# Turning the first nine and all half expert tiles on TensorE from whole rows, with another pace of the weight loads

## The chip, the cores and the metric

The kernel runs on one core of a Trainium2 chip. The metric is the device time of one execution in microseconds, as the median of three runs. The core's engines are TensorE (PE, with its weight loads as PEld), VectorE (DVE), ScalarE (ACT), GpSimd (POOL) and SyncE (SP); here SyncE issues nearly all ordinary DMAs and GpSimd the indirect ones.

## What is computed

Two layers in a row. The first is a long convolution over 4 sequences of 11456 tokens with 128 channels, done by Fourier transforms of length 2 x 11456 and multiplied by `x`. Its output, 45824 rows of 128, goes into a mixture of 8 experts, where each token takes the one expert with the highest logit:

```python
logits = x @ w_gate + modality_bias[modality_id]
e_idx = np.argmax(logits, axis=1)
probs = softmax(logits); gate_w = probs[np.arange(N), e_idx]
for e in range(E):                      # E = 8, D = 128, F = 1024
    mask = e_idx == e
    h = np.maximum(x[mask] @ w1[e], 0.0)
    out[mask] = gate_w[mask, None] * (h @ w2[e])
```

All of it is in fp32.

## The kernel before

The first half of the time (up to about 1100 us) is the convolution, with the routing of each sequence running one sequence behind. The routing puts each token's row into `xs` in HBM, sorted by expert. A row of `xs` has `RW = 130` numbers: 128 channels, the gate and the token's number. GpSimd writes these rows with indirect DMAs (`send_rows`, L269), and keeps doing so into the second half for the later sequences.

The second half is `experts(0, 99)` (L981). It goes over 99 tiles: 82 of `T = 512` rows, then 17 of `TH = 256` rows, the half tiles (up to five more half tiles lie behind a condition that does not hold with these inputs). Each tile belongs to one expert, which is read from a table at run time. The loop body is one chunk (`at`): a full tile has eight chunks `c`, a half tile four. In each chunk the order of the program, which is also the order of each engine's queue for TensorE, ScalarE, VectorE and SyncE, is: rows of tile `i + 2` are loaded if `c` is 0 (`rows_in`), `hidden(at)`, whole weights if due, one quarter of the weights of tile `i + 1` (`weights`, `c < 4`), `result(at - 3)`, and at fixed chunks `rows_turn(i + 1)`, `rows_split(i + 1)` and `rows_out(i - 1)`. GpSimd's order is found by the compiler's own planning.

- fp32 products are made of three matmuls on halves of the number, a high part (`h`, fp32r) and a low part (`l`, the rest). `weights` (L1049) makes them: ScalarE casts to `wh` (L1069), VectorE subtracts to `wl` (L1071); for half tiles the subtractions of parts 1 and 3 go to GpSimd. For the first `NDYN = 8` tiles the raw weights of the tile's expert are loaded just for it (`w1r`, `w2r`, L1028 and L1030, two buffers each); from tile 8 on they come from `w1a`, `w2a`, all experts' weights kept in SBUF, which `whole_weights` (L1041) loads in 16 DMAs of 512 KB, one in each odd chunk from tile 2 on.
- `rows_in` loads 512 rows so that VectorE's 32 x 32 transpose (L1088) gives channels on partitions: four DMAs in runs of 32 numbers (L1005), and one of the two last numbers of each row into `ends` (L1007). `rows_split` makes `xh` (ScalarE, L1096) and `xl` (VectorE, L1097).
- `hidden` makes `ph` (L1110 to L1112), then the relu `hh` on ScalarE (L1115) and `hl` on VectorE (L1116). `result` adds up `po` (L1133 to L1135) over the tile. After the last chunk VectorE transposes `po` to `oT` (L1141), four DMAs store it in short runs to `ob` in HBM (L1145), and one DMA reads it back as rows, `y` (L1147).
- `rows_out` casts the token numbers (`idx`, L1156), multiplies `y` by the gate on GpSimd (L1163) and scatters the rows to `out` by indirect DMAs, 128 rows each (L1165). Only the last tile is turned back by TensorE: `oT` by ScalarE (L1139), `pe.transpose` (L1160), the product on VectorE (L1161).

PSUM has eight banks, taken in turn by `bank(...)`. `x` and `ot` have four buffers, `ends` eight. `finale` (the end of the last routing) runs in tiles 0 and 1.

Of the kernel before, what the change touches and what calls it, by code (L numbers as in the profile page):

```python
# [12 lines left out]
F32 = mybir.dt.float32  # L13
# [22 lines left out]
B, S, D, E, F = 4, 11456, 128, 8, 1024  # L36
# [7 lines left out]
T = 512  # L44
# [11 lines left out]
RW = D + 2  # L56
# [11 lines left out]
TG, FL = 18, 2  # L68
NDYN = 8
NA, NXO = 11, 3  # L70


def places():
# [106 lines left out]
def hyena_moe_kernel(ctx: ExitStack, tc: tile.TileContext, a: dict, out: bass.AP,  # L180
                     nb: int = B, nt: int = NF + NH):
    nc = tc.nc
    pe, act, dve, pool, sp = nc.tensor, nc.scalar, nc.vector, nc.gpsimd, nc.sync
# [14 lines left out]
    def bank(name):  # L198
        return banks[-1].tile([D, 512], F32, tag="ps", name=name)
# [781 lines left out]
    def experts(lo, hi):  # L981
# [3 lines left out]
        last = hi - 1  # L985

        def rows_in(i):
            if i > last:
                return
            tb, col, n = tiles[i]  # L990
            for gen in {"1": (), "b": (second,)}.get(tb, (second, others)):
                for _ in gen:
                    pass
            tab = tabs[tb]
            r = nc.values_load(tab[0:1, 0, col:col + 1], engines=[ENG.SP], min_val=0, max_val=E * R,
                               skip_runtime_bounds_check_because="clamped above")
            k = kept[i] = {"n": n}

            x = k["x"] = mt.tile([D, T // 32, 32], F32, tag="x", name="x", bufs=4)
            ends = k["ends"] = mt.tile([D, 4, 2], F32, tag="ends", name="ends", bufs=8)  # L1000

            def rows():

                of = xs[ds(r, n), 0:D].rearrange("(f t) (k e) -> k t f e", t=32, e=32)
                lds = [sp.dma_start(x[32 * j:32 * j + 32, 0:n // 32], of[j]) for j in range(4)]  # L1005
                way = "(j p) r -> p j r" if i == last else "(p j) r -> p j r"
                lds.append(sp.dma_start(ends[:, 0:n // D],  # L1007
                                        xs[ds(r, n), D:RW].rearrange(way, j=n // D)))
                if tb in ("1", "b"):

                    known = max(nb - (2 if tb == "1" else 1), 0) * NR // D
                    assert len(scatters) >= known
                    for ld in lds:
                        for s in scatters[known:]:
                            tc.declare_no_dep(ins_of(ld), s, reason="rows of later tiles")
                        after_all(ld, scatters[:known])

            def raw_weights():

                e = nc.values_load(tab[0:1, 2, col:col + 1], engines=[ENG.SP], min_val=0, max_val=E - 1,  # L1020
                                   skip_runtime_bounds_check_because="clamped above")
# [12 lines left out]
            for part in of[:1] + [rows] + of[1:] if i == 0 else [rows] + of:  # L1034
                part()
            if i < NDYN:
                k["w", 1] = k["w", 1].rearrange("p c d -> p (c d)")
            if i == NDYN:
                whole_weights(2 * E)
# [9 lines left out]
        def weights(i, part):  # L1049
# [17 lines left out]
            else:  # L1067
                src = wv[m][:, ds(k["e"] + at, half)]
            act.copy(k[m, "h"][:, at:at + half], src)  # L1069
            eng = pool if k["n"] < T and part % 2 else dve  # L1070
            eng.tensor_sub(k[m, "l"][:, at:at + half], src, k[m, "h"][:, at:at + half].bitcast(F32))  # L1071

        def turn_tiles(i):

            k = kept[i]
            k["idx"] = mt.tile([D, 4], I32, tag="idx", name="idx", bufs=10)
            k["xT"] = mt.tile([D, T], F32, tag="xT", name="xT")
            k["xh"] = mt.tile([D, T], F32R, tag="xh", name="xh")
            k["xl"] = mt.tile([D, T], F32R, tag="xl", name="xl")

        def rows_turn(i):
            if i > last:
                return
            k = kept[i]
            n = k["n"]
            if "idx" not in k:
                turn_tiles(i)
            dve.transpose(k["xT"][:, 0:n], k["x"].rearrange("p f e -> p (f e)")[:, 0:n])  # L1088

        def rows_split(i):  # L1090
            if i > last:
# [27 lines left out]
        def result(at):  # L1119
# [15 lines left out]
                pe.matmul(po, k[1, "h"][:, f], hl[:, t], start=False, stop=g == NCH - 1)  # L1135
            if g == NCH - 1:
                oT = k["oT"] = mt.tile([D, T], F32, tag="oT", name="oT")
                if i == last:
                    act.copy(oT[:, 0:n], po)  # L1139
                    return  # L1140
                dve.transpose(oT[:, 0:n], po)  # L1141
                ob = ob_t[i % 4]
                to = ob[0:n].rearrange("(f t) (k e) -> k t f e", t=32, e=32)
                for j in range(4):
                    sp.dma_start(to[j], oT[32 * j:32 * j + 32, 0:n].rearrange("p (f e) -> p f e", e=32))  # L1145
                y = k["y"] = mt.tile([D, 4, D], F32, tag="y", name="y", bufs=2)
                sp.dma_start(y[:, 0:n // D], ob[0:n].rearrange("(p j) d -> p j d", j=n // D))  # L1147

        def rows_out(i):
            if not lo <= i <= last:  # L1150
# [1 line left out]
            k = kept.pop(i)  # L1152
            n = k["n"]
            ot = mt.tile([D, T], F32, tag="ot", name="ot", bufs=4).rearrange("p (j d) -> p j d", d=D)
            gate = k["ends"][:, 0:n // D, 0:1].broadcast_to([D, n // D, D])
            pool.tensor_copy(k["idx"][:, 0:n // D], k["ends"][:, 0:n // D, 1])  # L1156
            if i == last:
                pt = bank("pt")
                for j in range(n // D):
                    pe.transpose(pt[:, D * j:D * j + D], k["oT"][:, D * j:D * j + D], ident)  # L1160
                dve.tensor_mul(ot[:, 0:n // D], pt[:, 0:n].rearrange("p (j d) -> p j d", d=D), gate)  # L1161
            else:
                pool.tensor_mul(ot[:, 0:n // D], k["y"][:, 0:n // D], gate)  # L1163
            for j in range(n // D):
                s = pool.indirect_dma_start(  # L1165
                    out=out, out_offset=bass.IndirectOffsetOnAxis(ap=k["idx"][:, j:j + 1], axis=0),
# [10 lines left out]
        for at in range(len(work) + 6):  # L1177
# [9 lines left out]
                fetched.append(fetch(nb - 1))  # L1187
            if lo == 0 and 3 * at % 10 < 3:
                send_rows(1)
            if lo == 0 and 2 <= i and c % 2:  # L1190
                whole_weights(1)
            if 8 <= i < NW0:
                next(second, 0)
# [3 lines left out]
                weights(i + 1, c)  # L1197
            result(at - 3)
            whole = i <= last and tiles[i][2] == T
            if c == (3 if whole else 0):  # L1200
                rows_turn(i + 1)
            if c == (4 if whole else 1):
                rows_split(i + 1)
            if c == (5 if whole else 3):
                rows_out(i - 1)
# [50 lines left out]
```

## Time and profile before

| | us |
|---|---|
| median of 3 runs (2195.53 to 2204.09) | 2199.9 |
| the profiled execution | 2179.15 |
| its span, first to last instruction | 2177.3 |

| engine | busy, us | share of the span |
|---|---|---|
| PE | 2053.4 | 94% |
| PEld | 1662.4 | 76% |
| DVE | 1720.4 | 79% |
| ACT | 1183.9 | 54% |
| POOL | 1236.6 | 57% |

The share of busy time is an average over stages. The expert tiles are therefore read one by one: a tile lasts from its first `ph` matmul (L1110) to the next tile's, and the trace is cut there. In the view by stretches, a line gives the stretch in us from the span's start, its length, then for PE, PEld, DVE, ACT and POOL the busy time and in brackets the number of instructions, then the granted share of TensorE's clock (1.00 is 2.4 GHz, 0.5 would be 1.2 GHz throughout), the mean busy share of the 16 DMA engines and the GB/s that they moved. In the view of waits, a line names who waited, for whom, the total in us, how many times and the longest. In the timeline a line has the start, the length, engine, source line, operation, out<-in, how many were merged, and in square brackets the idle time before it and what ended it.

### The profile page before, as it was taken

The numbers are of one execution on the slowest core, as the hardware profiler recorded it, in microseconds if no ns is written. First come the engines' busy times: TensorE is split into PE (matmuls) and PEld (weight loads), VectorE is DVE, ScalarE is ACT, GpSimd is POOL, SyncE is SP. The second block draws the span as 40 slices with busy tenths as digits, with TensorE's granted clock in tenths as the row PEclk, the third lists the DMA queues.
The fourth block names the chain that finished last, engine by engine and source line by source line (L and its number), as shares of the span: only waits on it lengthen the run. The fifth ranks groups of instructions, "written<-read, shape, count | busy, mean of one in ns | idle before, by whom it ended". The sixth has DMA issues, their size and how long they took to land. (4 is left out here: it accounts for less than half of the span.)

```text
span 2177.3 us, 50618 instructions
## 1 busy us (share of the span) xinstructions
PE 2053.4 (94%) x18024; PEld 1662.4 (76%) x18024; DVE 1720.4 (79%) x2813; ACT 1183.9 (54%) x2155; POOL 1236.6 (57%) x1263
## 2 busy tenths in 40 slices
PE   8989999899989999899986899999999999999985
PEld 8878777677767777686565688888888888888884
DVE  2349777896789767996884899998899998889873
ACT  4642366225642366225653666666666666666653
POOL 0216400596448854596434578777777465554785
PEclk9999999999999999999998999999999999999997
DMA  9577677777878788785688766666665555555432
GB/s 313 219 286 229 236 231 217 236 256 271 303 258 271 269 284 302 247 263 164 191 197 225 174 134 133 127 125 131 124 130 116 114 102 98 98 97 94 81 69 54
DMA packets 592747, 406.51 MB, mean 187 GB/s; under 512 B 455977, under 2 KB 489469, under 8 KB 592489
## 3 DMA queue, kind: packets, MB, share of 16 engines
q1 hardware_dynamic: 565833, 343.82, 58.6%
q0 software_dynamic: 26496, 59.36, 7.9%
q8 instruction: 144, 2.36, 0.5%
q14 instruction: 114, 0.93, 0.1%
q10 hardware_dynamic: 160, 0.03, 0.0%
HBM read 295.03 MB, written 108.42 MB: 185 GB/s over the span
## 5 line engine op out<-in xcount | busy, mean ns | idle before, releaser
L1116 DVE SCALAR_TENSOR_TENSOR hl<-ph,hh 128x512 fp32r<-128x512 f32 x724 | 480.0, 675 | 74.4 <-ACT hh L1115 67.6
L269 POOL DMA_INDIRECT xs<-back,to x360 | 369.8, 1027 | 257.9 <-DVE y L675 83.0
L1115 ACT ACTIVATE hh<-ph 128x512 fp32r<-128x512 f32 x724 | 423.0, 598 | 168.3 <-PE ph L1112 161.8
L1165 POOL DMA_INDIRECT out<-ot,idx x362 | 400.9, 1107 | 110.4 <-issue 76.9
L1133 PE MATMUL po<-hh,wh 128*128 128x512 f32 (+1 forms) x792 | 297.2, 375 | 22.9 <-ACT hh L1115 22.9
L1110 PE MATMUL ph<-xh,wh 128*128 128x512 f32 (+1 forms) x792 | 297.4, 376 | 17.5 <-ACT xh L1096 17.5
L1112 PE MATMUL ph<-xl,wh 128*128 128x512 f32 (+1 forms) x792 | 297.4, 376 | 2.1 <-DVE xl L1097 2.1
L1134 PE MATMUL po<-hh,wl 128*128 128x512 f32 (+1 forms) x792 | 295.9, 374 | 2.9 <-POOL wl L1071 2.9
L1135 PE MATMUL po<-hl,wh 128*128 128x512 f32 (+1 forms) x792 | 296.3, 374 | 1.4 <-DVE hl L1116 1.1
L1111 PE MATMUL ph<-xh,wl 128*128 128x512 f32 (+1 forms) x792 | 296.3, 374 | 0.7 <-POOL wl L1071 0.7
L643 ACT COPY A<-pw 128x512 f32<-128x512 f32 (+1 forms) x184 | 97.1, 579 | 347.3 <-PE pw L639 347.3
L615 DVE TENSOR_TENSOR part<-pz,rings 128x1024 f32<-128x1024 f32 (+1 forms) x184 | 211.4, 1189 | 1.7 <-POOL part L620 1.7
L610 POOL TENSOR_TENSOR more<-more 128x256 f32<-128x256 f32 (+1 forms) x92 | 72.5, 788 | 233.1 <-DVE more L608 228.9
L639 PEld LDWEIGHTS pw<-rings,part 64*128 64x128 f32 x2880 | 175.5, 188 | 35.2 <-issue 28.4
L639 PE MATMUL pw<-rings,part 64*128 64x128 f32 x2880 | 200.3, 278 | 2.0 <-POOL part L620 1.9
L1163 POOL TENSOR_TENSOR ot<-y,ends 128x512 f32<-128x512 f32 (+1 forms) x98 | 104.4, 1065 | 167.7 <-DMA y<-ob 166.7
L596 PE MATMUL pz<-A,rings 128*64 128x256 f32 x1440 | 177.9, 389 | 15.1 <-DMA rings<-in_c_b 9.1
L1133 PEld LDWEIGHTS po<-hh,wh 128*128 128x128 f32 x792 | 151.2, 191 | 50.5 <-ACT hh L1115 24.6
L1110 PEld LDWEIGHTS ph<-xh,wh 128*128 128x128 f32 x792 | 151.1, 191 | 44.4 <-ACT xh L1096 19.1
L464 PE MATMUL s<-fwd,seq 128*64 128x90 f32 x4096 | 170.7, 242 | 6.0 <-issue 4.6
L1112 PEld LDWEIGHTS ph<-xl,wh 128*128 128x128 f32 x792 | 151.0, 191 | 30.7 <-DVE xl L1097 4.9
L1135 PEld LDWEIGHTS po<-hl,wh 128*128 128x128 f32 x792 | 150.7, 190 | 30.2 <-DVE hl L1116 4.6
(182 smaller groups left out, 3742.4 us busy)
## 6 DMA issues: line engine op xcount, KB each, us to landing
rings<-hs SPq DMA_DIRECT2D x88, 512.0 KB
seq<-in_u SPq DMA_DIRECT2D x64, 512.0 KB
seq<-in_v SPq DMA_DIRECT2D x64, 512.0 KB
seq<-in_x SPq DMA_DIRECT2D x64, 512.0 KB
xr<-xo SPq DMA_DIRECT2D x64, 365.6 KB
back<-xr SPq DMA_DIRECT2D x72, 325.0 KB
rings<-in_c_b SPq DMA_DIRECT2D x88, 256.0 KB
rings<-in_c_c SPq DMA_DIRECT2D x88, 256.0 KB
```

The lines of the kernel that those rows point to most:

```text
L269: s = pool.indirect_dma_start(out=xs, out_offset=bass.IndirectOffsetOnAxis(ap=ix, axis=0), in_=src, in_offset=None, bounds_check=E * R - 1 ...
L615: dve.tensor_mul(part[i], z[:, :, i].unsqueeze(1).broadcast_to([D, 2, n, 2, D]), h[:, 0].unsqueeze(3).broadcast_to([D, 2, n, 2, D]))
L639: pe.matmul(pw[par][:, to:to + D], t[at], k["c"][at, q, c], start=i == 0, stop=i == len(terms) - 1)
L1110: pe.matmul(p, k[0, "h"][:, f:f + D], k["xh"], start=True, stop=False)
L1111: pe.matmul(p, k[0, "l"][:, f:f + D], k["xh"], start=False, stop=False)
L1112: pe.matmul(p, k[0, "h"][:, f:f + D], k["xl"], start=False, stop=True)
L1115: act.activation(hh, ph, AF.Relu)
L1116: dve.scalar_tensor_tensor(hl, ph, 0.0, hh.bitcast(F32), op0=ALU.max, op1=ALU.subtract)
L1133: pe.matmul(po, k[1, "h"][:, f], hh[:, t], start=g == 0, stop=False)
L1134: pe.matmul(po, k[1, "l"][:, f], hh[:, t], start=False, stop=False)
L1135: pe.matmul(po, k[1, "h"][:, f], hl[:, t], start=False, stop=g == NCH - 1)
L1165: s = pool.indirect_dma_start(out=out, out_offset=bass.IndirectOffsetOnAxis(ap=k["idx"][:, j:j + 1], axis=0), in_=ot[:, j, :], in_offset=N ...
```

## The change

`NPE = 9`. A tile is `by_pe` if it is one of the first nine, the last, or a half tile. For such a tile:

- its rows are loaded whole, 130 numbers each, in one DMA into `x` (`[D, 4, RW]`), and `ends` is a part of that tile;
- `rows_turn` has TensorE transpose `x` (four or, in a half tile, two transposes of 128 x 128 with the identity) into a PSUM bank `px`, from which `rows_split` reads;
- `po` is copied to `oT` by ScalarE, transposed by TensorE into `pt` in `rows_out`, and multiplied by the gate on VectorE. `ob` and `y` are not used.

The other tiles, 9 to 81, do as before. For half tiles only part 3 of the low weights is on GpSimd (it was 1 and 3); their `rows_turn` is in chunk 1 (it was 0) and `rows_split` in chunk 2 (it was 1). The whole weights are loaded in chunks 0, 3 and 6 from tile 1 on.

```diff
+NPE = 9
...
-            x = k["x"] = mt.tile([D, T // 32, 32], F32, tag="x", name="x", bufs=4)
-            ends = k["ends"] = mt.tile([D, 4, 2], F32, tag="ends", name="ends", bufs=8)
+            by_pe = k["by_pe"] = i < NPE or i == last or n < T
+            x = mt.tile([D, 4, RW], F32, tag="x", name="x", bufs=4)
+            if by_pe:
+                k["x"], k["ends"] = x, x[:, :, D:RW]
+            else:
+                k["x"] = x.rearrange("p j r -> p (j r)")[:, 0:T]
+                k["ends"] = mt.tile([D, 4, 2], F32, tag="ends", name="ends", bufs=8)
...
+                by_token = xs[ds(r, n), :].rearrange("(p j) r -> p j r", j=n // D)
+                if by_pe:
+                    lds = [sp.dma_start(x[:, 0:n // D], by_token)]
+                else:
+                    of = xs[ds(r, n), 0:D].rearrange("(f t) (k e) -> k t f e", t=32, e=32)
+                    to = k["x"].rearrange("p (f e) -> p f e", e=32)
+                    lds = [sp.dma_start(to[32 * j:32 * j + 32], of[j]) for j in range(4)]
+                    lds.append(sp.dma_start(k["ends"], by_token[:, :, D:RW]))
...
-            eng = pool if k["n"] < T and part % 2 else dve
+            eng = pool if k["n"] < T and part == 3 else dve
...
-            dve.transpose(k["xT"][:, 0:n], k["x"].rearrange("p f e -> p (f e)")[:, 0:n])
+            if k["by_pe"]:
+                k["xT"] = bank("px")
+                for j in range(n // D):
+                    pe.transpose(k["xT"][:, D * j:D * j + D], k["x"][:, j, 0:D], ident)
+            else:
+                dve.transpose(k["xT"], k["x"])
...
-                if i == last:
+                if k["by_pe"]:
                     act.copy(oT[:, 0:n], po)
                     return
...
-            if i == last:
-                pt = bank("pt")
+            if k["by_pe"]:
+                pt = bank("pt").rearrange("p (j d) -> p j d", d=D)
                 for j in range(n // D):
-                    pe.transpose(pt[:, D * j:D * j + D], k["oT"][:, D * j:D * j + D], ident)
-                dve.tensor_mul(ot[:, 0:n // D], pt[:, 0:n].rearrange("p (j d) -> p j d", d=D), gate)
+                    pe.transpose(pt[:, j], k["oT"][:, D * j:D * j + D], ident)
+                dve.tensor_mul(ot[:, 0:n // D], pt[:, 0:n // D], gate.broadcast_to([D, n // D, D]))
             else:
-                pool.tensor_mul(ot[:, 0:n // D], k["y"][:, 0:n // D], gate)
+                pool.tensor_mul(ot, k["y"], gate.broadcast_to([D, 4, D]))
...
-            if lo == 0 and 2 <= i and c % 2:
+            if lo == 0 and 1 <= i and c % 3 == 0:
                 whole_weights(1)
...
-            if c == (3 if whole else 0):
+            if c == (3 if whole else 1):
                 rows_turn(i + 1)
-            if c == (4 if whole else 1):
+            if c == (4 if whole else 2):
                 rows_split(i + 1)
```

## Rows read from the trace of the kernel before

**Rows 1.** Busy time by stretch, cut at tiles; columns explained above.

```profile
1100.01:1113.79 13.78, 13.78 (x71) 10.48 (x72) 11.90 (x22) 10.45 (x21) 3.46 (x4) 0.88 0.95 245
...
1113.79:1126.29 12.50, 11.75 (x53) 9.07 (x52) 11.14 (x27) 6.19 (x12) 2.69 (x3) 1.00 0.76 200
...
1148.32:1168.05 19.73, 12.70 (x49) 9.72 (x48) 9.45 (x16) 7.07 (x15) 8.17 (x9) 0.83 0.86 222
...
1168.05:1190.46 22.41, 13.81 (x50) 10.71 (x48) 10.49 (x18) 7.76 (x15) 7.37 (x8) 0.77 0.87 227
...
1190.46:1208.78 18.32, 12.67 (x49) 9.91 (x48) 8.24 (x15) 6.38 (x13) 8.10 (x9) 0.81 0.89 225
...
1233.71:1244.59 10.88, 10.88 (x49) 9.01 (x48) 10.35 (x22) 6.91 (x14) 8.97 (x9) 1.00 0.76 152
...
1908.27:1951.79 43.52, 43.52 (x193) 36.05 (x192) 38.84 (x60) 29.44 (x53) 24.68 (x24) 1.00 0.53 98
...
2064.14:2069.89 5.75, 5.75 (x50) 5.75 (x49) 5.75 (x8) 3.58 (x8) 5.28 (x7) 1.00 0.39 55
...
2027.95:2144.47 116.52, 101.40 (x760) 96.92 (x759) 89.10 (x140) 71.35 (x142) 95.47 (x103) 0.96 0.39 75
```

**Rows 2.** Waits in tiles 3 to 7: total us, times, longest.

```profile
ACT wh L1069 <- DMA w1r<-in_moe_w: 34.6, 4, 12.2
...
PE po L1133 <- ACT hh L1115: 22.9, 4, 8.6
```

**Rows 3.** SyncE's own waits in tiles 3 to 7, same columns.

```profile
SPq L1147 <- DMA ob<-oT: 20.0, 7, 4.6
```

**Rows 4.** Timeline, tile 5: SyncE, then ScalarE; start, us, instruction, [idle before].

```profile
1170.38 6.43 SPq L1005 DMA_DIRECT2D x<-xs  x4
...
1177.97 0.40 SPq L1028 DMA_DIRECT2D w1r<-in_moe_w  x1
...
1181.79 0.62 ACT L1069 CAST wh<-w1r 128x512 fp32r<-128x512 f32 x1 [12.25 <-DMA w1r<-in_moe_w]
```

**Rows 5.** Timeline, last half tiles: SyncE, then VectorE.

```profile
2140.06 1.87 SPq L1005 DMA_DIRECT2D x<-xs  x4
...
2142.12 0.40 SPq L1007 DMA_DIRECT2D ends<-xs  x1
...
2142.57 1.94 SPq L1145 DMA_DIRECT2D ob<-oT  x4
...
2143.54 0.45 DVE L1088 STREAM_TRANSPOSE xT<-x 128x256 f32<-128x256 f32 x1 [2.12 <-DMA x<-xs]
```

**Rows 6.** Groups by form, half tiles: busy us, mean ns, idle before.

```profile
L1116 DVE SCALAR_TENSOR_TENSOR hl<-ph,hh 128x512 fp32r<-128x512 f32 x63 | 40.9, 666 | 3.8 <-ACT hh L1115 3.1
...
L1071 DVE TENSOR_TENSOR wl<-w2a,wh 128x512 fp32r<-128x512 f32 x15 | 16.8, 1123 | 0.3 <-ACT wh L1069 0.3
...
L1088 DVE STREAM_TRANSPOSE xT<-x 128x256 f32<-128x256 f32 x16 | 7.0, 440 | 23.7 <-DMA x<-xs 23.7
...
L1141 DVE STREAM_TRANSPOSE oT<-po 128x256 f32<-128x256 f32 x14 | 6.2, 441 | 0.0
```

**Rows 7.** Timeline of TensorE where four fp32 transposes stand among matmuls.

```profile
1112.65 0.60 PE L727 MATMUL lt<-ident,oT 128*109 128x128 f32 x4
...
1113.32 0.39 PE L1134 MATMUL po<-hh,wl 128*128 128x512 f32 x1
```

**Rows 8.** Timeline of the tail: ScalarE, VectorE, GpSimd.

```profile
2152.90 0.37 ACT L1139 COPY oT<-po 128x256 f32<-128x256 f32 x1 [2.28 <-PE po L1135]
...
2153.86 0.42 DVE L1161 TENSOR_TENSOR ot<-pt,ends 128x256 f32<-128x256 f32 x1 [2.51 <-PE pt L1160]
...
2157.62 0.61 POOL L1163 TENSOR_TENSOR ot<-y,ends 128x256 f32<-128x256 f32 x1 [1.02 <-SPq L1214]
...
2161.10 0.97 POOL L1165 DMA_INDIRECT out<-ot,idx  x1 [0.30 <-POOLq L1214]
...
2162.38 0.97 POOL L1165 DMA_INDIRECT out<-ot,idx  x1 [0.30 <-issue]
```

More of the change, by code (lines that the diff above doesn't have):

```diff
@@ L997, in rows_in @@
             k = kept[i] = {"n": n}
-            x = k["x"] = mt.tile([D, T // 32, 32], F32, tag="x", name="x", bufs=4)
-            ends = k["ends"] = mt.tile([D, 4, 2], F32, tag="ends", name="ends", bufs=8)
-            def rows():
[L1004 to L1008, printed above, removed]
+            by_pe = k["by_pe"] = i < NPE or i == last or n < T
[5 more added lines that the diff above has]
+                k["ends"] = mt.tile([D, 4, 2], F32, tag="ends", name="ends", bufs=8)
+            def rows():
+                by_token = xs[ds(r, n), :].rearrange("(p j) r -> p j r", j=n // D)
[6 more added lines that the diff above has]
+                    lds.append(sp.dma_start(k["ends"], by_token[:, :, D:RW]))
                 if tb in ("1", "b"):
@@ L1076, in turn_tiles @@
             k["idx"] = mt.tile([D, 4], I32, tag="idx", name="idx", bufs=10)
-            k["xT"] = mt.tile([D, T], F32, tag="xT", name="xT")
+            if not k["by_pe"]:
+                k["xT"] = mt.tile([D, T], F32, tag="xT", name="xT")
             k["xh"] = mt.tile([D, T], F32R, tag="xh", name="xh")
@@ L1137, in result @@
                 oT = k["oT"] = mt.tile([D, T], F32, tag="oT", name="oT")
-                if i == last:
+                if k["by_pe"]:
                     act.copy(oT[:, 0:n], po)
                     return
-                dve.transpose(oT[:, 0:n], po)
+                dve.transpose(oT, po)
                 ob = ob_t[i % 4]
-                to = ob[0:n].rearrange("(f t) (k e) -> k t f e", t=32, e=32)
+                to = ob.rearrange("(f t) (k e) -> k t f e", t=32, e=32)
                 for j in range(4):
-                    sp.dma_start(to[j], oT[32 * j:32 * j + 32, 0:n].rearrange("p (f e) -> p f e", e=32))
-                y = k["y"] = mt.tile([D, 4, D], F32, tag="y", name="y", bufs=2)
-                sp.dma_start(y[:, 0:n // D], ob[0:n].rearrange("(p j) d -> p j d", j=n // D))
+                    sp.dma_start(to[j], oT[32 * j:32 * j + 32].rearrange("p (f e) -> p f e", e=32))
+                k["y"] = mt.tile([D, 4, D], F32, tag="y", name="y", bufs=2)
+                sp.dma_start(k["y"], ob.rearrange("(p j) d -> p j d", j=4))
         def rows_out(i):
@@ L1154, in rows_out @@
             ot = mt.tile([D, T], F32, tag="ot", name="ot", bufs=4).rearrange("p (j d) -> p j d", d=D)
-            gate = k["ends"][:, 0:n // D, 0:1].broadcast_to([D, n // D, D])
+            gate = k["ends"][:, 0:n // D, 0:1]
             pool.tensor_copy(k["idx"][:, 0:n // D], k["ends"][:, 0:n // D, 1])
-            if i == last:
-                pt = bank("pt")
+            if k["by_pe"]:
+                pt = bank("pt").rearrange("p (j d) -> p j d", d=D)
                 for j in range(n // D):
-                    pe.transpose(pt[:, D * j:D * j + D], k["oT"][:, D * j:D * j + D], ident)
-                dve.tensor_mul(ot[:, 0:n // D], pt[:, 0:n].rearrange("p (j d) -> p j d", d=D), gate)
+                    pe.transpose(pt[:, j], k["oT"][:, D * j:D * j + D], ident)
+                dve.tensor_mul(ot[:, 0:n // D], pt[:, 0:n // D], gate.broadcast_to([D, n // D, D]))
             else:
-                pool.tensor_mul(ot[:, 0:n // D], k["y"][:, 0:n // D], gate)
+                pool.tensor_mul(ot, k["y"], gate.broadcast_to([D, 4, D]))
             for j in range(n // D):
```

## The prediction, made before the changed kernel was built or run

> **What bounds the kernel now.** I read the windows cut at the first `ph` matmul of each expert tile first [rows 1]. From tile 9 to tile 81 a tile takes 10.88 us with TensorE busy throughout, which is 48 matmuls at 0.227 us: there TensorE alone sets the time, and what the change does not touch cannot move. Two stretches are not like that. The first nine tiles run from 1100.01 to 1233.71, 133.7 us where nine dense ones would be 97.9. The sixteen half tiles before the last one run from 2027.95 to 2144.47, 116.5 us, while a half tile that does not wait takes 5.75. After TensorE's last work there is a tail on GpSimd.
>
> In the first stretch the loss sits in tiles 4 to 6 (19.7, 22.4 and 18.3 us, DMA engines 0.86 to 0.89 busy, granted clock 0.77 to 0.83). The table of waits names it [rows 2]: ScalarE waits 34.6 us in four waits for `w1r`, its relu is queued behind that cast, and TensorE waits 22.9 us for the relu. The timeline of tile 5 shows why `w1r` is late [rows 4]: tile 5 began at 1168.05, and only in it does SyncE issue the rows that stand in the program at the head of tile 4. Their four issues take 6.43 us (64 KB each in runs of 128 bytes), and `w1r` goes out at 1177.97 and is cast at 1181.79, so its own trip is only 3.8 us. SyncE also stands still 20.0 us before `y<-ob`, until the `ob` stores have landed [rows 3]. So the bound is SyncE's order, filled by the round trip `oT`, `ob`, `y` and by transfers in short runs.
>
> In the half tiles it is the same queue without the weights [rows 5]: the rows of the last tile are issued at 2140.06, though the program asks for them at the head of tile 96, two tiles ahead; one tile's turn on SyncE is 1.87 us for `x`, 0.40 for `ends`, 1.94 for `ob`, and the wait for the store. VectorE waits 23.7 us for `x` in ten waits [rows 6], and the next tile's first matmul waits for what follows from it.
>
> **The change part by part.** *Transposes on TensorE.* Each of the nine full tiles gets 8, each half tile 4; the last tile had its two output ones already. That is 72 and 66. Price: four fp32 transposes between fp32r matmuls start at 1112.65, and the second matmul behind them starts at 1113.32 [rows 7]; 0.67 less one matmul's 0.227 is 0.44, so 0.11 each. They all lie on the path: 7.9 us in the first stretch, 7.3 in the half tiles.
>
> The Trainium skill, "TensorE: Matmul & The Clock Gate", Part 4, says that such a transpose took about 275 ns in one kernel's context. If that were its cost on the engine, 138 of them would be 38 us instead of 15; the rows that show the spacing speak for 15, and the other case is a rival below.
>
> *What goes from SyncE and the DMA engines.* Per changed tile: four short-run `x` loads and `ends` become one load of 2080-byte rows, the four `ob` stores and `y` vanish, and with them both of SyncE's waits. SyncE then issues a tile's rows when the program asks for them. DMA time: a tile of nothing but rows is 10.88 x 0.53 = 5.8 us for 1.07 MB [rows 1]; tile 5 is 19.5 us for 5.1 MB; the difference is 3.4 us a MB, 1.8 us a weight load of 0.52 MB. At that rate `y` and `out` are 0.9 each and `x` with `ob` 4.0; after the change `x` is 0.9, so a tile saves 4.0 us of DMA time. With two raw and, in place of four, three whole weight loads a tile needs 5 x 1.8 + 0.9 + 0.9 + about 1.1 to 1.6 for the scatter of earlier rows (0.3 to 0.5 MB), 11.9 to 12.4 us, against 10.88 + 0.88 = 11.76 on TensorE. At the share of 0.95 that tile 0 reached, that is up to 1.3 us short a tile for five tiles, 6 us at most; but raw weights are issued a whole tile ahead of their cast and their trip was 3.8, so most of it is covered. I take 2.5 us, bounds 0 and 6.
>
> First stretch after: tiles 0 and 1 as now (13.78 and 12.50, they hold the end of routing), seven at 10.88, 7.9 of transposes, 2.5 of waits: 112.8. **Gain 20.9**, bounds 15 and 25 (the last if the 0.75 us that TensorE was idle in tile 1 and the slow clock of tile 0 go too).
>
> *Half tiles.* After: 5.75 + 0.44 = 6.19. Other engines, per half tile: VectorE is busy 89.10 / 16 = 5.57 now; it loses two transposes (0.44 each), gains one weight subtraction and the product with the gate (0.42, as the last tile's [rows 8]). The subtraction was 1.12 there [rows 6], beside GpSimd's own, but VectorE's `hl` of the same width is 0.67, so I take 0.7: 5.8, or some 5.3 if the two subtractions left on VectorE get shorter once GpSimd does one instead of two. ScalarE goes from 4.46 to 4.8 (the `oT` copy, 0.37 [rows 8]), GpSimd from 5.97 to about 4.0. None passes 6.19, but VectorE is near, and `xl` is now due only two chunks (2.9 us) ahead of its reader; I allow 0.15 a tile. 16 x 6.34 = 101.4. **Gain 15.1**, bounds 0 and 17.5. The later turn and split cost nothing as long as `x` comes early: it is issued at the head of the tile before, about 7 us ahead, and its trip, from the last issue at 2141.9 to VectorE's read at 2143.54, is under 2.
>
> *The tail.* TensorE's last product is multiplied by 2154.28 [rows 8]; GpSimd's last two scatters end at 2163.35, because tile 97 waits for `y` until 2157.62 and its two scatters stand ahead. Without `y` tile 97's are long out, and the last two need 2.6 us (1.28 from one scatter to the next, 0.3 ahead of the first): they end at 2156.9, 6.4 earlier. **Gain 6.2** after two more transposes, bounds 5 and 7.
>
> *At nothing:* the gate product moved to VectorE in the full tiles (TensorE has three chunks of slack ahead of a `hl`, and VectorE loses two transposes for it); the whole weights' other pace (they are first read in tile 7, the last is issued in tile 6); rows kept in `x` until GpSimd has read their ends (four buffers, needed two tiles later; if GpSimd were that late, SyncE would stand). TensorE now waits itself for `x`, with everything behind it: that is the rival on the other side.
>
> Sum 20.9 + 15.1 + 6.2 = 42. The profiled execution takes 2179.15 us, 1.85 more than its span of 2177.3, and 20.7 less than the median of the runs, 2199.9; I take that distance as fixed: 2137 for a profiled execution, **2158** for the median.
>
> **The rivals.** *DMA still bounds the first tiles.* For: the demand of 11.9 to 12.4 against 11.76. Against: SyncE no longer blocks, and the prefetch. The bulk then takes all of the 6 us and the slow clock stays; gain 10 there: 2169.
> *Half tiles stay at 7.3.* VectorE at 5.8 of 6.19 delays `xl` and the last `hl`, and a wait on VectorE takes the place of the one on `x`. For: dense half tiles already show VectorE busy for all of the 5.75 us. Against: less of GpSimd beside it. No gain there: 2173.
> *A transpose costs its whole duration.* Four last 0.60 from the first start to the last end [rows 7], so one alone lasts 0.60 - 3 x 0.11 = 0.27. If they do not overlap with the matmuls around them, because their data has only just come, 138 x 0.27 is 37 instead of 15: gain 20, 2180. Against: rows 7. The page's figure above says the same.
> *Slower: TensorE stands for `x`.* In place of VectorE, which had chunks of slack behind it, TensorE itself is held in its queue until the whole-row load has landed. At the longest wait seen, 3.2 us, on all 25 changed tiles: 80 lost, 42 gained, 2238. It decides from 2.1 us a tile (53 lost, 11 more than gained). Against: the load is one issue and early.
> *It does not do what it says:* the waits in front move from `ob` to another of SyncE's (buffers of `x`, raw weights), and only the tail is gained: 2194.
>
> **How the numbers follow.** Forecast 0.60 (2146 to 2166 by the bounds of its terms and the scatter of the runs, 4 us either way); DMA-bound 0.13; half tiles unchanged 0.14; transposes at full price 0.03; slower 0.05; only the tail 0.05. The range from 2146 to 2180 takes in the first four and leaves out about 0.15. A difference under 0.5%, 11 us, is about what a measurement here cannot tell from none. Faster 0.90, same 0.05, slower 0.05.
>
> **What would show it.** Right: tiles 2 to 8 at 11.8 us with a granted clock of 1.00; no ScalarE wait for `w1r` over 2 us; half tiles at 6.2 to 6.4 with VectorE busy some 0.87; tile 9 on at 10.88; the last scatter within 4 us of the last transpose. Wrong: tiles 4 to 7 over 13 us with the DMA share near 0.9 (first rival); half tiles at 7 with waits of the first matmul on `xl` or of the second product on `hl` (second); transposes 0.27 apart; TensorE's transposes of `x` waiting for its DMA. If tiles 9 to 81 change, the reading of the middle as bound by TensorE alone was wrong.

## The result, and the profile of the changed kernel

The changed kernel takes 2162.55 us (median of 4 runs, 2159.6 to 2171.82), the kernel before 2199.44 beside it: a ratio of 0.9839, with a 95% interval from 0.9803 to 0.9874, 36.9 us less. The forecast was 2158, from 2146 to 2180, with faster at 0.90. The profiled execution took 2161.77 us, its span 2160.0.

The two profiled executions can't be compared as wholes. ScalarE's last exponential of the routing, the last step ahead of the experts that both kernels share, stands at these times, first in the kernel before, then in the changed one (timeline of ScalarE):

```profile
1095.32 0.31 ACT L755 ACTIVATE powers<-lg 109x128 f32<-109x128 f32 x1 [5.17 <-DVE lg L753]
```

```profile
1113.35 0.31 ACT L756 ACTIVATE powers<-lg 109x128 f32<-109x128 f32 x1 [5.19 <-DVE lg L754]
```

Up to there the two programs differ only in the loads of the first tiles' rows, in the four transposes of tile 0's `x` and in a pair of matmuls that changed places, and yet 18.0 us lie between; over the other kernels below this point lies anywhere from 1093.9 to 1122.0. So the stages are compared from it on: to the end of the span it is 1082.0 us before and 1046.6 after, 35.4 less, which agrees with the medians. By stage, cut as before the prediction:

| us | before | after | gained | forecast |
|---|---|---|---|---|
| exponential to first `ph` | 4.7 | 1.4 | 3.3 | 0 |
| tiles 0 to 8 | 133.7 | 116.6 | 17.1 | 20.9 |
| tiles 9 to 81 | 794.2 | 795.0 | -0.7 | 0 |
| tiles 82 to 97 | 116.5 | 106.7 | 9.8 | 15.1 |
| tile 98 and tail | 32.9 | 27.0 | 5.9 | 6.2 |
| sum | 1082.0 | 1046.6 | 35.4 | 42 |

The 0.7 us in tiles 9 to 81 are transposes that fall there: four for tile 8's rows in tile 9 (11.35 us) and two for tile 82's in tile 81 (11.15); all tiles between them take 10.88 as before.

Windows of the changed kernel, columns as before: tiles 0, 3, 5, 6 and 7, a dense half tile, tiles 83 to 86 together, and all sixteen half tiles, to be read beside [rows 1]:

```profile
1114.70:1131.54 16.84, 15.56 (x75) 11.45 (x75) 13.16 (x29) 10.73 (x21) 4.10 (x4) 0.80 0.64 199
...
1156.44:1168.26 11.82, 11.82 (x57) 9.80 (x56) 9.04 (x14) 7.70 (x15) 5.50 (x7) 1.00 1.07 365
...
1180.08:1192.21 12.13, 12.13 (x57) 9.64 (x56) 7.05 (x11) 6.76 (x14) 7.37 (x9) 1.00 0.89 300
1192.21:1204.09 11.88, 11.88 (x57) 9.79 (x56) 10.40 (x18) 8.03 (x15) 7.86 (x10) 1.00 0.38 109
1204.09:1219.91 15.82, 13.89 (x57) 10.68 (x56) 8.93 (x15) 7.98 (x15) 6.14 (x7) 0.89 0.27 61
...
2081.74:2088.10 6.36, 6.36 (x56) 6.22 (x54) 5.38 (x11) 4.98 (x11) 3.47 (x4) 1.00 0.15 42
...
2032.13:2062.62 30.49, 25.99 (x211) 24.91 (x209) 24.18 (x39) 19.67 (x41) 25.39 (x29) 1.00 0.25 66
...
2026.26:2132.99 106.73, 102.22 (x823) 98.93 (x821) 88.34 (x143) 78.63 (x159) 68.15 (x77) 1.00 0.18 52
```

Tiles 4 to 6, 18 to 22 us before, now take 11.8 to 12.1 with TensorE busy throughout at a granted clock of 1.00. A tile is called dense here if TensorE never idles in it. Behind tiles 0 and 1 two places are not dense: tile 7, at 15.8 where 11.8 would do, and the half tiles 83 to 86, at 30.5 where four dense ones take 25.5. In the waits of tiles 3 to 7, ScalarE's for `w1r` is gone, and of TensorE's for the relu [rows 2] one of 1.9 us in tile 7 is left. SyncE's wait for the `ob` stores [rows 3] is gone too, and another stands in its place, for a buffer of `x` that VectorE's product with the gate still reads:

```profile
SPq L1016 <- DVE ot L1176: 17.2, 2, 9.8
SPq L1012 <- DVE ot L1176: 16.7, 3, 9.2
```

It costs no tile anything that the windows show: tiles 3 to 6 are dense beside it. In the tail the first of the last two scatters starts 1.7 us behind the start of the last transposes (2142.00); before, tile 97's product and scatters, which had waited for `y`, stood ahead of them [rows 8] (timeline of GpSimd):

```profile
2143.67 0.98 POOL L1180 DMA_INDIRECT out<-ot,idx  x1 [0.98 <-issue]
2144.96 0.98 POOL L1180 DMA_INDIRECT out<-ot,idx  x1 [0.30 <-POOLq L1229]
```

### The profile page after: what moved, and what is told of

It reads as the page before. It is cut to its first block, busy times and chain, and to the rows that moved or that the text cites. A ratio compares the mean times of both kernels' runs of the same rounds, so it can differ in the third digit from the quotient of the medians.

```text
span 2160.0 us, 50351 instructions
## 1 busy us (share of the span) xinstructions
PE 2070.0 (96%) x18162; PEld 1673.0 (77%) x18162; DVE 1712.3 (79%) x2804; ACT 1191.0 (55%) x2180; POOL 1195.6 (55%) x1221
## 5 line engine op out<-in xcount | busy, mean ns | idle before, releaser
L640 PEld LDWEIGHTS pw<-rings,part 64*128 64x128 f32 x2880 | 176.2, 188 | 35.4 <-issue 27.1
L597 PE MATMUL pz<-A,rings 128*64 128x256 f32 x1440 | 182.4, 397 | 14.5 <-DMA rings<-in_c_b 11.7
L1127 PEld LDWEIGHTS ph<-xl,wh 128*128 128x128 f32 x792 | 149.5, 189 | 32.2 <-DVE xl L1112 3.9
L1125 PEld LDWEIGHTS ph<-xh,wh 128*128 128x128 f32 x792 | 149.6, 189 | 30.5 <-ACT xh L1111 5.6
L465 PEld LDWEIGHTS s<-fwd,seq 128*64 128x64 f32 x4096 | 161.9, 137 | 14.7 <-issue 6.4
L1126 PEld LDWEIGHTS ph<-xh,wl 128*128 128x128 f32 x792 | 149.8, 189 | 27.0 <-DVE wl L1080 1.8
```

The costliest lines, as they stand in the source:

```text
L465: pe.matmul(v[64 * c:64 * c + 64, blk, j], u[:, blk, 4 * h + j], fwd[:, c], start=True, stop=True)
L640: pe.matmul(pw[par][:, to:to + D], t[at], k["c"][at, q, c], start=i == 0, stop=i == len(terms) - 1)
L1125: pe.matmul(p, k[0, "h"][:, f:f + D], k["xh"], start=True, stop=False)
L1126: pe.matmul(p, k[0, "l"][:, f:f + D], k["xh"], start=False, stop=False)
L1127: pe.matmul(p, k[0, "h"][:, f:f + D], k["xl"], start=False, stop=True)
```

## The experiments

Each variant is an edit of the changed kernel unless it says otherwise. All by stage, cut in the same way; the ratio is to the kernel before, run beside it.

| us | to first `ph` | 0 to 8 | 9 to 81 | 82 to 97 | tail | sum | ratio [95%] |
|---|---|---|---|---|---|---|---|
| before | 4.7 | 133.7 | 794.2 | 116.5 | 32.9 | 1082.0 | 1 |
| changed kernel | 1.4 | 116.6 | 795.0 | 106.7 | 27.0 | 1046.6 | 0.9839 [0.9803, 0.9874] |
| the same again | 1.4 | 117.3 | 795.3 | 106.7 | 27.0 | 1047.6 | 0.9838 [0.9811, 0.9865] |
| half tiles undone | 1.4 | 116.9 | 800.9 | 118.2 | 31.7 | 1069.0 | 0.9898 [0.9865, 0.9931] |
| first tiles undone | 4.7 | 130.0 | 800.1 | 107.4 | 27.0 | 1069.2 | 0.9924 [0.9894, 0.9953] |
| old pace | 1.4 | 112.4 | 795.5 | 107.1 | 27.0 | 1043.4 | 0.9805 [0.9775, 0.9834] |
| GpSimd's share undone | 1.4 | 115.8 | 801.1 | 118.2 | 27.1 | 1063.5 | 0.9874 [0.9842, 0.9906] |
| GpSimd's share alone | 4.7 | 131.5 | 797.7 | 116.0 | 33.6 | 1083.6 | 0.9989 [0.9972, 1.0007] |
| no share for GpSimd | 1.4 | 116.6 | 795.0 | 107.7 | 26.9 | 1047.6 | 0.9832 [0.9801, 0.9862] |
| way out only | 4.7 | 107.0 | 805.0 | 106.6 | 26.4 | 1049.7 | 0.9847 [0.9814, 0.9879] |
| way in only | 1.4 | 124.3 | 800.9 | 133.2 | 32.2 | 1092.0 | 1.0013 [0.9993, 1.0033] |
| transposes of `x` three times | 1.4 | 118.9 | 795.6 | 111.7 | 27.0 | 1054.5 | 0.9864 [0.9832, 0.9897] |
| way out, old pace | 4.7 | 106.1 | 794.7 | 107.1 | 26.4 | 1039.0 | 0.9816 [0.9789, 0.9843] |
| the same, tiles 79 to 81 too | 4.7 | 106.1 | 795.7 | 98.4 | 26.4 | 1031.2 | 0.9774 [0.9747, 0.9802] |

### Each half of the change undone

The half tiles as they were, but for the last tile's way out:

```diff
-            by_pe = k["by_pe"] = i < NPE or i == last or n < T
+            by_pe = k["by_pe"] = i < NPE
+            out_pe = k["out_pe"] = i < NPE or i == last
...
-            eng = pool if k["n"] < T and part == 3 else dve
+            eng = pool if k["n"] < T and part % 2 else dve
...
-            if c == (3 if whole else 1):
+            if c == (3 if whole else 0):
```

`rows_split` goes back by a chunk too. Here and below, `out_pe` takes the place of `by_pe` where `po` is copied, transposed and multiplied.

> The changed kernel (2162.6 us median; its first nine tiles 116.6 us, its sixteen half tiles 106.7, the stretch behind them 27.0) with the half tiles done the old way: rows in short runs, turned by VectorE, out by ob and y, low weights 1 and 3 on GpSimd, turn and split one chunk earlier. My theory, SyncE's queue bounds the half tiles: they go back to 115 to 117 us, the stretch behind them to 32 to 33, the first nine stay at 115 to 118; 15 us in all, 2178. Rival, the freed DMA engines and queue of the first tiles shift the whole second half, so that the half tiles had little to do with it: under 5 us, 2167 or less.

Measured: 2183.2 us. The first nine tiles keep their 116.9, the half tiles and the tail go back to 118.2 and 31.7. The median is 5 us above mine. Tile 9 takes 17.0 us in the profiled execution where 11.35 is dense; but the kernel before, run beside it, took 2205.27, 5.8 more than beside the changed kernel, so that by the ratio no excess is left.

The first nine tiles as they were:

```diff
-NPE = 9
+NPE = 0
```

> The changed kernel with the first nine full tiles turned by VectorE from short runs and put out by ob and y; the new pace of the whole weights and the half tiles stay as changed. My theory, the row traffic and SyncE's waits bound the first tiles: nine tiles at 128 to 134 us instead of 116.6, with ScalarE waits for w1r of 5 us and more; 2175 to 2180. Rival, the spread of the whole weights over six tiles did it: nine tiles at 113 to 119, 2159 to 2166 (they are then even spared 7.9 us of transposes).

Measured: 2188.79 us, the first nine tiles 130.0, in my range; the median is 9 us above it, of which tiles 9 and 10 (12.5 and 14.2 us) are 5, and the kernel before took 2205.27 on this occasion too. The new pace alone gives at most 3.7 us in the first nine tiles. The wait over tiles 4 to 7 is that of [rows 2]:

```profile
ACT wh L1078 <- DMA w1r<-in_moe_w: 25.2, 3, 9.4
```

So both halves of the change gain by themselves, and the pace is not what brings the first nine tiles down.

### The pace, and the stall in tile 7

```diff
-            if lo == 0 and 1 <= i and c % 3 == 0:
+            if lo == 0 and 2 <= i and c % 2:
```

> The changed kernel with the old pace of the whole weights: from tile 2 on, in every odd chunk, four a tile. My theory: the DMA engines, which moved 300 to 365 GB/s in tiles 2 to 5 of the changed kernel, carry this too; nine tiles at 116 to 123 us, up to 2168. Rival, the pace is what helped: the waits for w1r come back, nine tiles at 127 or more, 2173 or more.

Measured: 2162.49 us. The first nine tiles take 112.4, shorter than with the new pace, and tile 7 is dense (windows, that variant):

```profile
1208.58:1220.41 11.83, 11.83 (x58) 9.80 (x56) 7.81 (x12) 7.48 (x15) 7.94 (x9) 1.00 0.38 90
```

In the changed kernel the stall looks like this (timeline of tile 7, one line each of SyncE, ScalarE, VectorE, TensorE and GpSimd):

```profile
1203.03 3.51 SPq L1016 DMA_DIRECT2D x<-xs  x3
...
1208.93 0.60 ACT L1130 ACTIVATE hh<-ph 128x512 fp32r<-128x512 f32 x1 [5.31 <-PE ph L1127]
1209.56 0.69 DVE L1131 SCALAR_TENSOR_TENSOR hl<-ph,hh 128x512 fp32r<-128x512 f32 x1 [5.21 <-issue]
...
1209.58 0.50 PE L1148 MATMUL po<-hh,wh 128*128 128x512 f32 x1 [1.93 <-issue]
...
1210.38 0.97 POOL L270 DMA_INDIRECT xs<-back,to  x1 [1.89 <-issue]
```

The `ph` that ScalarE's relu reads was complete at 1203.6, and the relu runs 5.3 us later. VectorE's `hl` and TensorE's `po` read what the relu writes and start right behind it; GpSimd goes on with its scatters until 1208.49 and stands only then, for 1.89 us. TensorE is idle 1.93 us, and the tile's granted clock falls to 0.89, which is the rest of the 4.0 us that the tile is longer than a dense one. The kernel run once more, unaltered, showed whether that was an accident:

> The changed kernel once more, unaltered, as a control for the stalls seen in its profile. Theory: the stall in tile 7 (15.8 us where 11.35 would be dense) belongs to this order of the transfers and comes again at the same place; from the last exponential of the routing to the end 1046 to 1048 us, median 2160 to 2165. The rival: it was an accident of one profiled execution; tile 7 at 11.4 to 11.9 and 1041 to 1043 us to the end.

Measured: 2162.77 us, 1047.6 to the end, and the stall at the same place (windows):

```profile
1200.51:1217.71 17.20, 14.29 (x57) 10.61 (x56) 9.06 (x15) 7.96 (x15) 6.01 (x8) 0.90 0.24 55
```

So the stall belongs to the kernel and not to one execution. It is absent from the three edits of the changed kernel that have the old pace; most of those with the new pace have it, in tile 7, in tile 9 or in both, and the one with the threefold transposes (below) has it in neither. So the pace brings it about, with the rest of the order. The medians are too coarse to show it: 2162.49 us without the stall, 2162.55 and 2162.77 with it, and the intervals of the ratios overlap. What the relu stands for is not settled: no wait on a transfer or on another engine's instruction accounts for it, and in the view of the DMA queues for 1203 to 1220 none loads instructions.

### Which way matters, in or out

Only the way out over TensorE; the rows come in by four short-run loads and VectorE:

```diff
-            by_pe = k["by_pe"] = i < NPE or i == last or n < T
+            by_pe = k["by_pe"] = False
+            out_pe = k["out_pe"] = i < NPE or i == last or n < T
```

> As the changed kernel, but only the way out goes over TensorE (po copied, transposed, multiplied by the gate; no ob, no y); the way in is the old one: four loads in runs of 128 bytes and ends, turned by VectorE. My theory, that SyncE's standing before y until the ob stores have landed is what made the rows and the raw weights late: most of the gain stays. First nine tiles 118 to 124 us (before 133.7, changed kernel 116.6), sixteen half tiles 104 to 110 (116.5, 106.7), tail 27; median 2163 to 2172. The rival, that the short-run loads of x themselves (6.43 us of issues a tile, low DMA rate) are the cause: first nine tiles 125 to 132, half tiles 111 or more, median 2175 to 2188.

Measured: 2164.6 us, the first nine tiles 107.0, less than the changed kernel's and less than either expectation, with every tile from 2 to 6 at 11.35. What it wins there it loses in tile 9, 21.7 us long by a stall of the kind shown above (ScalarE idles 7.3 us before a relu).

Only the way in:

```diff
             by_pe = k["by_pe"] = i < NPE or i == last or n < T
+            out_pe = k["out_pe"] = i == last
```

> The mirror of the run before: whole rows in and turned by TensorE, but the way out over ob and y as in the kernel before (the last tile's excepted). My theory, that SyncE standing before y is the cause: the waits for the ob stores come back; first nine tiles 124 to 133 us, half tiles 110 or more, tail 31 to 33, median 2176 to 2192. The rival, that the short-run loads of x were the cause: first nine tiles 116 to 122, half tiles 104 to 109, tail 32 all the same, median 2166 to 2173.

Measured: 2204.78 us, no gain in all, and worse than either expectation. The first nine tiles, 124.3, are in my range, 5.7 us less than with neither way changed and the same pace (130.0, first tiles undone). SyncE's waits there (tiles 4 to 7) and in ten half tiles (88 to 97):

```profile
SPq L1165 <- DMA ob<-oT: 12.7, 5, 5.6
SPq L1013 <- POOL ot L1181: 6.4, 4, 1.8
```

```profile
SPq L1013 <- POOL ot L1181: 36.0, 10, 5.1
SPq L1165 <- DMA ob<-oT: 12.2, 18, 1.4
```

The wait for `ob` is back. The 36.0 us in the half tiles are this variant's own: `x` holds the gates, so its buffer stays until GpSimd has multiplied `y`, and the next load waits for it. So its half tiles (8.0 us each) say nothing on the short-run loads; that its tail is 32.2 again does say that the tail's gain comes of the way out.

The verdict: taking out the round trip over `ob` is enough by itself for the first tiles; the whole-row loads and the transposes of `x` aren't needed beside it and cost 0.48 us a full tile (11.83 against 11.35). Alone they take off a part of the loss, so the short runs of `x` had a share in filling SyncE's queue. The round trip was more than the wait of [rows 3]. Tile 5 of the kernel before (timeline of SyncE):

```profile
1179.75 3.56 SPq L1145 DMA_DIRECT2D ob<-oT  x4
...
1187.63 0.34 SPq L1147 DMA_DIRECT2D y<-ob  x1
```

From the first store's issue to the end of the load's issue SyncE is held 8.1 to 8.5 us in each of tiles 3 to 6, and 3.3 to 3.7 of that are the issues of the four stores. The edit takes out the issues, the wait, the transfers and GpSimd's product together; what each was worth is not told apart.

### What a transpose costs

```diff
-                for j in range(n // D):
+                for j in 3 * list(range(n // D)):
                     pe.transpose(k["xT"][:, D * j:D * j + D], k["x"][:, j, 0:D], ident)
```

> As the changed kernel, but each transpose of x is done three times over into the same place: 140 more (8 in a full tile, 4 in a half tile), nothing else. If a transpose costs its spacing, 0.11 us: full tiles 2 to 6 at 12.7 us (11.83 in the changed kernel), dense half tiles at 6.81 (6.37), in all 15 us more, median 2175 to 2181. The rival, that it costs its whole duration, 0.27: full tiles at 14.0, half tiles at 7.45, 38 us more, median 2198 to 2204.

Measured: a full and a dense half tile (windows):

```profile
1142.43:1155.14 12.71, 12.71 (x65) 10.66 (x64) 9.23 (x14) 7.80 (x15) 4.40 (x5) 1.00 1.07 342
...
2082.45:2089.27 6.82, 6.82 (x60) 6.69 (x58) 5.39 (x11) 4.99 (x11) 3.48 (x4) 1.00 0.13 39
```

Eight more cost 0.87 in a full tile (11.84 without), four 0.46 in a half tile: 0.11 each, as [rows 7] had it. The median, 2168.41, is below both expectations: the stall of tile 7 is absent here (4.0 us), and tiles 83 to 86 lose 2.9 us and not 5.0. One transpose's own time in this variant is 0.27 us all the same (groups by form, tiles 0 to 8):

```profile
L1101 PE MATMUL px<-ident,x 128*128 128x128 f32 x96 | 11.8, 273 | 0.0
```

The Trainium skill, "TensorE: Matmul & The Clock Gate", Part 4, gives about 275 ns for a transpose in one kernel's context; the trace agrees with it as a duration, and this run shows that it is not the price among other matmuls.

### GpSimd beside VectorE in the half tiles

The share of GpSimd as before, all else changed:

```diff
-            eng = pool if k["n"] < T and part == 3 else dve
+            eng = pool if k["n"] < T and part % 2 else dve
```

> The changed kernel with low weights 1 and 3 of the half tiles on GpSimd again. My theory: GpSimd at some 5.3 us a half tile is no bound, VectorE gets 0.7 us less to do but its own subtractions are stretched more often; the dense half tile goes from 6.37 to between 6.2 and 6.7, sixteen of them 104 to 110, 2160 to 2166. Rival, GpSimd's relief is what made the half tiles faster: 7.0 us and more a tile, 113 or more, 2169 or more.

Measured: 2178.28 us; the sixteen half tiles take 118.2, no better than in the kernel before. The rival was right. The loss stands in tiles 83 to 85. VectorE's subtraction in tile 83, and GpSimd at the same time (timelines of the two):

```profile
2050.48 4.67 DVE L1080 TENSOR_TENSOR wl<-w1a,wh 128x512 fp32r<-128x512 f32 x1
```

```profile
2051.03 1.30 POOL L1080 TENSOR_TENSOR wl<-w2a,wh 128x512 fp32r<-128x512 f32 x1
2052.28 1.31 POOL L1080 TENSOR_TENSOR wl<-w1a,wh 128x512 fp32r<-128x512 f32 x1
2053.53 1.05 POOL L1178 TENSOR_TENSOR ot<-y,ends 128x512 f32<-128x512 f32 x1
```

A subtraction of 0.69 us lasts 4.67: it ends 0.56 after the third of GpSimd's operations, which stand one behind the other. In tile 85 it is the other way: the cast for part 1 is done at 2068.86, GpSimd's subtraction of it starts only at 2071.67, behind scatters on its own queue, and TensorE waits for it (waits, half tiles):

```profile
PE ph L1126 <- POOL wl L1080: 4.2, 1, 4.2
```

The Trainium skill, "SBUF — State Buffer", section "Who interferes with whom", says that a VectorE instruction with two inputs in SBUF contends with a GpSimd instruction that reads SBUF, and calls the contention an exclusive lock. The 4.67 us agree with that, and go further: VectorE stood through three of GpSimd's operations in a row.

The same edit alone, on the kernel before:

```diff
-            eng = pool if k["n"] < T and part % 2 else dve
+            eng = pool if k["n"] < T and part == 3 else dve
```

> The kernel before with one edit alone: of the half tiles' weight subtractions only part 3 is on GpSimd (it was 1 and 3). Since the changed kernel without this edit gained nothing in the half tiles, the edit may be enough by itself. My theory: it is not, because here VectorE still waits for x behind SyncE's queue; sixteen half tiles 112 to 117 us (before 116.5), median 2195 to 2201. The rival, that GpSimd's subtractions were the whole loss of the half tiles: 104 to 109 us, median 2187 to 2192.

Measured: 2197.84 us and 116.0 for the half tiles: alone it gains nothing, since VectorE still waits for `x` [rows 6] (groups by form, half tiles):

```profile
L1088 DVE STREAM_TRANSPOSE xT<-x 128x256 f32<-128x256 f32 x16 | 7.1, 442 | 25.5 <-DMA x<-xs 25.5
```

So the half tiles had two limits, one behind the other, and both edits are needed. With no subtraction on GpSimd at all:

```diff
-            eng = pool if k["n"] < T and part == 3 else dve
+            eng = pool if k["n"] < T and False else dve
```

> As the changed kernel, but none of the half tiles' weight subtractions is on GpSimd (it had one of four). Theory that VectorE's subtraction is stretched while GpSimd subtracts too (0.69 us alone, up to 2.34 beside it), so that less of it is better down to nothing: tiles 83 to 86 lose their 5 us, sixteen half tiles 102 to 105 (changed kernel 106.7), median 2158 to 2163. The rival, that VectorE becomes the bound with the fourth subtraction (5.4 us busy of 6.36 in a dense half tile, plus 0.69, and its queue has no slack left for xl): sixteen half tiles 110 or more, over 6.8 a tile, median 2168 or more.

Measured: 2163.68 us, the half tiles 107.7, between the two expectations. A dense half tile takes 6.32, VectorE busy 5.82 of it, so VectorE is not the bound. Its subtractions are nearly even now, 0.71 us in the mean, where these were 1.28 with GpSimd's old share (groups by form, half tiles; first the variant without GpSimd, then the one with its old share):

```profile
L1080 DVE TENSOR_TENSOR wl<-w1a,wh 128x512 fp32r<-128x512 f32 x32 | 22.6, 706 | 0.0
```

```profile
L1080 DVE TENSOR_TENSOR wl<-w1a,wh 128x512 fp32r<-128x512 f32 x16 | 20.6, 1284 | 0.1
```

Yet tiles 85 and 86 lose 6.2 us, and not by stretched subtractions: the longest takes 1.48 us, and in tile 85 ScalarE idles 4.4 us before a relu and runs it late without a cause that the profile shows, as in tile 7. What of GpSimd's larger operations on SBUF is left there are its products of `y` with the gate for tiles 79 to 81, 1.05 us each, which run into the half tiles. Taking these away was tried last, on the kernel that follows.

### A version that is faster than both

The way out alone, and the old pace of the whole weights:

```diff
-            by_pe = k["by_pe"] = i < NPE or i == last or n < T
+            by_pe = k["by_pe"] = False
+            out_pe = k["out_pe"] = i < NPE or i == last or n < T
...
-            if lo == 0 and 1 <= i and c % 3 == 0:
+            if lo == 0 and 2 <= i and c % 2:
```

> Only the way out over TensorE, as in the run of that name, and the whole weights in each odd chunk from tile 2 on, as in the kernel before. Theory: the stall of some 10 us in tile 9 of the run with the way out alone goes with the whole weights' pace, as the one of tile 7 did; first nine tiles 106 to 110 us, tile 9 at 10.9 to 11.5, median 2152 to 2159, better than the changed kernel. The rival: the stall comes of something else, and tiles 7 to 9 lose 4 to 11 us again; median 2161 to 2167. A third way: with the old pace and the short-run loads the raw weights come late again, tiles 4 to 6 at 13 us or more.

Measured: 2158.85 us. All tiles from 2 to 9 take 11.35 and no stall is left in them; the ratio's interval overlaps the changed kernel's, the time from the routing's last exponential is 7.6 us shorter. The third way did not come, though `x` comes in short runs and the DMA share is 1.09, as the view counts it, the highest of the tiles shown (windows, tile 6):

```profile
1190.41:1201.77 11.36, 11.36 (x54) 9.42 (x53) 8.61 (x14) 7.79 (x15) 6.83 (x8) 1.00 1.09 344
```

On top of that, tiles 79 to 81 out over TensorE:

```diff
-            out_pe = k["out_pe"] = i < NPE or i == last or n < T
+            out_pe = k["out_pe"] = i < NPE or i >= 79
```

> The best kernel so far (only the way out over TensorE, the whole weights at the old pace) with the way out over TensorE in tiles 79 to 81 too, so that no product by the gate of a full tile is left on GpSimd when the half tiles begin. In that kernel tiles 82 to 86 take 38.7 us where five dense ones take 30.8. Theory: VectorE's two-input instructions stand while GpSimd reads SBUF, and in tiles 82 to 85 GpSimd's products of tiles 79 to 81 (1.05 us each) and the scatters behind y crowd them; tiles 82 to 86 at 32 to 35 us, sixteen half tiles 101 to 104 (was 107.1), three tiles 0.44 longer each, median 2153 to 2158. The rival: the loss there is the change from full to half tiles itself (twice the weights a time, xl due at once); sixteen half tiles 106 to 108, median 2157 to 2162.

Measured: 0.9774 [0.9747, 0.9802] of the kernel before, whose median beside it was 2175.27 us: 2127.18 us. The unchanged stage was shorter for both on that occasion (the exponential at 1093.9), so the ratio counts and not the time that was expected. The first five half tiles, which took 38.7 us, and all sixteen (windows):

```profile
2000.31:2030.91 30.60, 30.60 (x245) 29.71 (x243) 27.40 (x49) 24.59 (x50) 20.60 (x24) 1.00 0.23 44
2000.31:2098.73 98.42, 98.42 (x795) 96.05 (x793) 88.36 (x159) 79.75 (x160) 58.16 (x65) 1.00 0.21 40
```

TensorE is busy throughout, and the half tiles are 8.6 us shorter, more than the expected 3 to 6. The interval lies wholly below the changed kernel's, by a hair, and overlaps that of the version without this edit; that the half tiles are dense rests on the one profiled execution. So the loss at the head of the half tiles came from the way out of the three full tiles before them. The edit takes away their products on GpSimd and their `ob` and `y` transfers together; which of these it was is not told apart by this run. Stretched subtractions were the smaller part of it: without this edit VectorE's fifteen in tiles 82 to 86 run over 0.68 us each by 1.7 us together, the longest 1.91, while these tiles lose 7.9.

## Why the prediction was right, and where its sum was off

- **What bounds the kernel.** Right, as SyncE's order filled by the round trip: with the way out alone the first tiles are dense, with the way in alone the wait for `ob` and a part of the loss are back. The short runs of `x` alone do not bound them.
- **Transposes at 0.11 us.** Right, by the threefold run; the rival at 0.27 falls.
- **First nine tiles, 20.9 of gain forecast, 17.1 measured.** Three of its steps were off. The allowance of 2.5 us for DMA was not needed: the price of 3.4 us a MB from tile 5 [rows 1] counted a queue that stood, and tile 3 now moves 365 GB/s at a share of 1.07, as the view counts it, without a wait; the rival that DMA still bounds falls with it. Tiles 0 and 1 "as now" were 2.3 us over their twelve transposes: tile 0, at a granted clock of 0.80, not 0.88, takes 3.1 more. The first `ph` no longer waits behind VectorE, which saves 3.3 us ahead of tile 0 and was not in the forecast. And the whole weights' other pace, put "at nothing" because the last is issued ahead of its reader, costs 4.0 us in tile 7 of the profiled execution; how it holds ScalarE there stays open.
- **Half tiles, 15.1 forecast, 9.8 measured.** The dense tile, 6.34 forecast, is 6.37. The term was mis-sized by 5.0 us in tiles 83 to 86, and the step behind it failed: 0.15 us a tile was allowed alike for all sixteen, set against VectorE's mean busy time (5.3 or 5.8 of 6.19), and nothing for what the last full tiles, which go out as before, leave to GpSimd and SyncE when the half tiles begin. Of TensorE's 4.4 us of idling in tiles 83 to 86, 2.0 come where VectorE has just run subtractions of 2.34 and 1.77 us, the rest behind others of VectorE's instructions and a late relu; with tiles 79 to 81 out over TensorE too all of it is gone. GpSimd's relief, which the text entered as an effect on VectorE's busy time, decides whether anything is gained: without it the half tiles take 118.2. The rival "half tiles stay at 7.3" had named the engine but not the cause.
- **Tail, 6.2 forecast, 5.9 measured.** Right; the last scatter ends 3.5 us after the last transpose.
- **Slower, TensorE stands for `x`.** It did not come: in no tile does a transpose of `x` wait for its load. The cost "if GpSimd were that late" did come in another form, SyncE's 33.9 us for buffers of `x` that VectorE's product still reads, and it is covered.
- **The median from one profiled execution.** The step failed. The distance of 20.7 us, taken as fixed, lies in a stage that the change does not touch and goes with the occasion: the routing's last exponential stands at 1095.3 in that execution and at 1109.7 or later in all others but the last variant's, and beside that one the kernel before itself took 2175.27. The changed kernel's distance is 0.8. The forecast for a profiled execution, 2137, was missed by 25 us, and that of the median, 2158, only by 4.6, because there the distance cancels.

## What to carry to other kernels

A store to memory and its load back on one queue held up everything issued behind them; taking out that round trip was worth more than making the transfers beside it larger, and it was found by asking what the queue stands for, not by its busy share. Where two engines exclude each other, read the longest instruction and what ran beside it, not the busy time: an operation moved to a helper engine can hold up the one it was to relieve. And before a sum is set against a median, check on a step that both kernels share how far the profiled execution stands from the others.

## What was not expected of the hardware

- VectorE's subtraction of two SBUF operands, 0.69 us, lasted up to 4.67 us while GpSimd ran operations on SBUF back to back.
- With SyncE's wait for `ob` gone, the DMA engines moved 300 to 365 GB/s in tiles 2 to 5, against 222 to 227 in tiles 4 to 6 before [rows 1], and 344 with the short-run loads still among them (way out, old pace, tile 6).
- At the end of the stall in tile 85 of the variant without a share for GpSimd, three matmuls start 0.71 us apart with no wait that the profile names (timeline of TensorE); shortly before, in the same tile, they are 0.12 apart. What holds them there stays open, as for the stall of tile 7.

```profile
2055.30 0.28 PE L1125 MATMUL ph<-xh,wh 128*128 128x256 f32 x1 [0.93 <-issue]
2056.01 0.28 PE L1126 MATMUL ph<-xh,wl 128*128 128x256 f32 x1 [0.43 <-issue]
2056.72 0.57 PE L1127 MATMUL ph<-xl,wh 128*128 128x256 f32 x1 [0.43 <-issue]
```
